# A hand-set order of two engine queues in the middle product of a fused attention and two-MLP kernel: other due times, weight passes queued up to three granules ahead, other sums in the closing chain

## The chip, the cores and the metric

The kernel runs on one core of a Trainium2 chip. Five engines take part, each with a queue that it works through strictly in order: TensorE (PE, matrix products into PSUM), ScalarE (ACT), VectorE (DVE), GpSimd (POOL) and SyncE (SP, which only issues DMAs here). An instruction that waits for a semaphore holds up everything behind it on its engine. The metric is device time in microseconds (us) of one launch; lower is better.

## What is computed

```python
x = attention(q, k, v)                 # 2 x 12 heads, 448 tokens, head size 64, causal, fp32
x = reshape(x)                         # (896 tokens, 768)
y = ((x @ w_a) * (x @ w_b)) @ w_out    # 768 -> 1536 -> 768, the "moe" weights
h = y @ w_in                           # 768 -> 2048, the "moe2" weights
g = h * sigmoid(h)
out = (g @ w_out2).astype(float32)     # 2048 -> 768
```

All is fp32. The kernel keeps that accuracy by splitting each operand into a high and a low part of a narrower type (`fp32r`) and running three matmuls for each product: high x high, high x low, low x high.

## The kernel before

**Stages.** Attention comes first (to about 92 us), then stage 1 (`w_ab`, the two gate products), stage 2 (`w_mid`, the middle product), stage 3 (`w_in`) and stage 4 (`w_out`). A stage is a list of granules; a granule is a pair of 128-column output blocks, named by its first block m, and a plain granule is 72 matmuls long (12 for each of 6 chunks), a fast one 63. A fast granule does the product of a 2x2 block matrix with seven block products instead of eight (Winograd's form): block products 1, 2, 6, 5, 7, 3, 4 in this order, 9 matmuls each, on sums of activations `p1` to `p7` and sums of weights `wa`, `wb`, `wc`, `wd`, each as a high and a low half (`p5h`, `p5l`, `wbh`, `wbl`).

**The middle product** has six granules on PE in this order: plain m=0, plain m=2, fast m=0, plain m=4, fast m=2, fast m=4. Stage 3 follows with fast granules m=0, 2, 4 and on. A plain granule ends with four accumulators (`acc`, one PSUM bank each; there are 8 banks in all). Three of them stay in PSUM until the fast granule of the same m has added its part (`held`), the fourth is copied to SBUF (`o`). In a fast granule of stage 2 (`quad`, lines 897 to 955) block products 1, 6, 7 and 4 pile up in one bank `a`. After 1, after 6 and after 7 ScalarE copies the bank (`s1`, `s2`, `s3`, line 340), and PE may add the next product only when that copy has been made. VectorE adds the other banks to these copies (`plus`, line 921), which sets the banks free. In stage 3, which has no held banks, product 5 is copied as well (`s5`), before product 3 may use its bank.

**Weights.** A granule's weights arrive by two DMAs into three raw buffers `wr`. A raw buffer is loaded again only after VectorE has joined it. Each one passes ScalarE twice (lines 241 and 246) and VectorE once (line 252, `wq`, the join). A fast granule then takes four VectorE sums (lines 300 and 305, `wt`) and four pairs of halves: ScalarE makes the high one (line 274), VectorE the low one (line 278). There is one `wq` and one `wt` buffer, so a join waits for the last reader of the granule before.

**Activations of stage 3.** After fast m=0 and m=2 the sums `p3`, `p5`, `p6`, `p7` are made by `sums_mid` (lines 499 to 549: one sum at line 515, then halves at lines 520 and 521). After fast m=4, the last one, the last third of all `p` is made by `closing` (lines 345 to 395): sums at line 363, high halves on ScalarE at line 352, low halves on VectorE at line 355. Stage 3 m=0 needs it chunk by chunk as the third chunk of each block product.

**What sets the order.** Nothing is scheduled by a compiler here. The program is recorded once, and `Timeline` merges two things onto the ScalarE and VectorE queues: tasks that a product has put there with a delay counted in matmuls (`line.after`), and the weight steps of coming granules, each with a due time in matmuls from a table (`CONV_F`, and the hand-set `MID_2`, `MID_4`, `IN_0`, `IN_2`, `IN_4`). `line.convert` puts the weight steps of granule at+2 on this list when granule `at` begins. A time in the tables is in matmuls relative to the granule's own start (`at_mm`).

## Time and profile before

| what | value |
|---|---|
| median of 3 runs | 550.06 us (549.98 to 550.39) |
| the profiled execution | 550.08 us |
| its span, first to last instruction | 548.3 us |
| mean granted TensorE clock | 0.999 |
| PE busy | 538.6 us, 98% of the span |
| VectorE busy | 427.4 us, 78% |
| ScalarE busy | 388.2 us, 71% |
| middle product on PE (plain m=0 to the start of stage 3) | ends at 328.0 us |

The profile gives for each engine its busy time, the instructions in order of time with the idle time before each and what ended it, and who waited for whom. Matmul ends are modelled, so the idle time shown before a matmul is shorter than what PE lost there. The distance between the starts of neighbouring matmuls is the better measure: where nothing is late, one starts 0.20 us after the other.

### The profile page before, as it was taken

What the parts mean: (1) busy time and instruction counts of PE and PEld (TensorE: products, weight loads), DVE (VectorE), ACT (ScalarE), POOL (GpSimd) and SP (SyncE); (2) the same over time, 40 slices, a digit from 0 to 9 for tenths busy, and PEclk for the clock granted to TensorE, in tenths of its full rate; (3) what the DMA queues carried; (4) which work ended last, traced back from release to release, by engine and by line L of the source; (5) the groups of instructions that cost most, each with busy time, mean ns of one, the idle gap of its engine ahead of it and who ended that gap; (6) DMA issues with size and microseconds to landing.
All of it is one profiled execution on the core that took longest, in us unless ns stands there. A gap on an engine that the chain in (4) does not pass through costs nothing.

```text
span 548.3 us, 8421 instructions
## 1 busy us (share of the span) xinstructions
PE 538.6 (98%) x3016; PEld 469.8 (86%) x3016; DVE 427.4 (78%) x858; ACT 388.2 (71%) x727; POOL 47.8 (9%) x101
## 2 busy tenths in 40 slices
PE   9999999999999999999989998999999999999997
PEld 6566667999999999999978987999999999999996
DVE  5798897987877878999878799877765696475773
ACT  6999986766666666887675657987776897375631
POOL 4565570000000000000000000000000000000000
PEclk9999999999999999999999999999999999999999
DMA  7574340333333334426343303334433233622022
GB/s 224 167 273 120 134 154 3 108 123 115 117 115 116 115 126 139 144 62 205 91 157 116 116 1 109 121 122 137 144 93 139 68 124 104 222 84 91 18 100 86
DMA packets 17226, 65.82 MB, mean 120 GB/s; under 512 B 3616, under 2 KB 5152, under 8 KB 17184
## 3 DMA queue, kind: packets, MB, share of 16 engines
q1 hardware_dynamic: 17184, 65.28, 36.0%
q8 instruction: 24, 0.39, 0.3%
q14 instruction: 18, 0.15, 0.1%
HBM read 62.52 MB, written 2.75 MB: 119 GB/s over the span
## 4 chain that ended last, share of the span: by engine, by line
PE 90%; DVE 5%; ACT 2%; DMA 1%; issue 1%; SPq 0%; ACTq 0%
PE acc L317 77%; PE xo L781 4%; PE pt L770 4%; PE sc L696 3%; PE sc L707 2%; DMA v<-v 1%; DVE s L921 1%; PE wp L799 1%; DVE wq L252 0%; SPq L672 0%; DVE wt L300 0%; DVE S L515 0%; ACT wr L246 0%; ACT wr L241 0%; DVE wal L278 0%
## 5 line engine op out<-in xcount | busy, mean ns | idle before, releaser
L340 ACT COPY s<-acc 128x448 f32<-128x448 f32 x93 | 49.5, 533 | 81.7 <-PE acc L317 81.1
L252 DVE SCALAR_TENSOR_TENSOR wq<-wr 128x768 uint32<-128x768 uint32 (+1 forms) x70 | 65.2, 933 | 20.8 <-ACT wr L246 20.8
L246 ACT ACTIVATE wr<-wr,wbias 128x768 uint32<-128x768 uint32 (+1 forms) x70 | 68.3, 975 | 0.0
L241 ACT ACTIVATE wr<-wr 128x768 f32<-128x768 f32 (+1 forms) x70 | 62.6, 894 | 0.0
L727 ACT ACTIVATE p<-sm,nmax 128x256 f32<-128x256 f32 (+3 forms) x84 | 43.9, 528 | 7.8 <-DVE nmax L722 6.7
L739 POOL TENSOR_SCALAR p<-p,rcp 128x256 f32<-128x256 f32 (+3 forms) x84 | 45.1, 555 | 33.8 <-DVE rcp L736 23.5
L722 DVE CUSTOM_DVE_ANT_0 sm<-sc,mask 128x256 f32<-128x256 f32 (+3 forms) x84 | 30.5, 416 | 7.6 <-PE sc L696 4.5
L913 DVE TENSOR_TENSOR s<-acc,s 128x448 f32<-128x448 f32 x42 | 26.0, 620 | 9.3 <-PE acc L317 9.3
L278 DVE TENSOR_TENSOR wbl<-wt,wbh 128x768 fp32r<-128x768 f32 x24 | 23.0, 957 | 12.0 <-ACT wbh L274 12.0
L278 DVE TENSOR_TENSOR wcl<-wt,wch 128x768 fp32r<-128x768 f32 x24 | 23.0, 956 | 11.5 <-ACT wch L274 11.4
L317 PE MATMUL acc<-th,wgbh 128*128 128x448 f32 x96 | 27.6, 366 | 1.0 <-DVE s L921 1.0
L317 PE MATMUL acc<-th,wgah 128*128 128x448 f32 x96 | 27.6, 367 | 0.8 <-DVE s L921 0.8
L317 PE MATMUL acc<-p6h,wch 128*128 128x448 f32 x72 | 26.5, 367 | 1.4 <-ACT s L340 1.4
L317 PE MATMUL acc<-tl,wgbh 128*128 128x448 f32 x96 | 27.4, 366 | 0.0
L317 PE MATMUL acc<-th,wgal 128*128 128x448 f32 x96 | 27.4, 366 | 0.0
L317 PE MATMUL acc<-tl,wgah 128*128 128x448 f32 x96 | 27.3, 366 | 0.0
L317 PE MATMUL acc<-th,wgbl 128*128 128x448 f32 x96 | 27.3, 366 | 0.0
L305 DVE TENSOR_TENSOR wt<-wq,wt 128x384 f32<-128x384 f32 x48 | 26.6, 555 | 0.8
L770 PEld LDWEIGHTS pt<-ident,p 128*128 128x128 f32 x192 | 20.5, 141 | 7.6 <-POOL p L739 6.0
L770 PE MATMUL pt<-ident,p 128*128 128x128 f32 x192 | 26.7, 280 | 0.3 <-POOL p L739 0.3
L317 PE MATMUL acc<-p3h,wdh 128*128 128x448 f32 x72 | 26.3, 366 | 0.5 <-ACT s L340 0.5
L317 PE MATMUL acc<-p7h,wbh 128*128 128x448 f32 x72 | 26.4, 367 | 0.1
(205 smaller groups left out, 1532.9 us busy)
## 6 DMA issues: line engine op xcount, KB each, us to landing
wr<-w_ab SPq DMA_DIRECT2D x24, 768.0 KB, 4.6
wr<-w_in SPq DMA_DIRECT2D x16, 768.0 KB, 4.5
wr<-w_mid SPq DMA_DIRECT2D x12, 768.0 KB, 4.4
wr<-w_out SPq DMA_DIRECT2D x12, 768.0 KB, 4.8
qk<-qk SPq DMA_DIRECT2D x12, 448.0 KB, 5.0
v<-v SPq DMA_DIRECT2D x12, 256.0 KB, 4.3
wr<-w_out SPq DMA_DIRECT2D x6, 512.0 KB, 4.4
out<-o SPq DMA_DIRECT2D x12, 224.0 KB, 1.9
```

What stands on the lines that cost most here:

```text
L241: nc.scalar.activation(out=w, in_=w, func=AF.Prelu, scale=2.0 ** -112, alpha=-(2.0 ** 32))
L246: nc.scalar.activation(out=word(i, 0), in_=word(i, 0), func=AF.Relu, bias=wbias, scale=2.0 ** -29)
L252: nc.vector.scalar_tensor_tensor(out=xi(i), in0=word(i, 1), scalar=3, in1=word(i, 0), op0=ALU.logical_shift_left, op1=ALU.bitwise_or)
L278: nc.vector.tensor_tensor(out=view[1], in0=src(), in1=view[0].bitcast(F32), op=ALU.subtract)
L305: nc.vector.tensor_tensor(out=sums(1, k), in0=tile(1 - k, 1), in1=sums(k, 0), op=ALU.subtract)
L317: nc.tensor.matmul(out=acc[:, 0:S], lhsT=w, rhs=a, start=first, stop=last, skip_group_check=True)
L340: nc.scalar.copy(out=t, in_=acc[:, 0:S])
L722: nc.vector.tensor_tensor_reduce(out=sm[:, o:o + m.shape[-1]], in0=sc, in1=m, op0=ALU.add, op1=ALU.min, scale=-(D ** -0.5), scalar=nmax, a ...
L727: nc.scalar.activation(out=p_sb[u % 2][j][:, 0:K], in_=sm[:, 0:K], func=AF.Exp, bias=t["nmax"][:, c:c + 1], scale=-1.0, accum_out=t["sums" ...
L739: nc.gpsimd.tensor_scalar(out=pj, in0=pj, scalar1=t["rcp"][:, COL[j]:COL[j] + 1], scalar2=1.0, op0=ALU.mult, op1=ALU.mult,)
L770: nc.tensor.transpose(out=out_, in_=p, identity=ident)
L913: nc.vector.tensor_tensor(out=t, in0=bank[:, 0:S], in1=other, op=ALU.add)
```

## The change

Three parts, all in how the two queues are filled; no arithmetic instruction is added or removed except that one sum of the closing chain goes another way, with the same count of instructions on every engine.

1. The due times of five weight tables are other ones, and plain m=4 of stage 2 gets a table of its own (`MID_P`).
2. The weight steps of stage 3 m=0 and m=2 are queued up to three granules ahead (`ahead`) instead of two.
3. `sums_mid` makes the sums in another order (S1, S2, S3, S4), and the halves with them. In `closing` three sums stood between the last copy and S2's first half (held part to s3, s3 minus s1, held part off s1); now the held part is taken off s1 as soon as s1 is there, s3 minus s1 follows alone, and the held part goes to s3 at the end.

```diff
-MID_2 = at_mm(72, exp=(-52, -34), low=(-48, -30), join=(-24, -20), t13=-16, t24=-12,
-              wa=(-14, -8), wd=(-10, -5), wc=(-6, 0), wb=(2, 6))
+MID_P = at_mm(63, exp=(-20, -12), low=(-15, -8), join=(-7, -2), ghi=(0, 4), glo=(5, 9))
+MID_2 = at_mm(72, exp=(-50, -42), low=(-46, -34), join=(-40, -29), t13=-24, t24=-16,
+              wa=(-13, -4), wd=(-9, 4), wc=(1, 10), wb=(5, 14))
...
             if (i, j) == (0, 0):
+
+                def part_of():
+                    op(t, t, h[3], ALU.subtract)
                 line.after(3, partial(halves_of, t, 1))
+                line.after(8, part_of)
             elif (i, j) == (0, 1):
-                halves_of(t, 2, 2)
+                f["rest2"] = halves_of(t, 2, None)
             elif (i, j) == (1, 1):
-                halves_of(t, 4)
-
-                def ahead():
-                    a11, part = f[0, 0], h[3]
-                    op(t, part, t, ALU.add)
-                    f["S2"] = A.new(F32, "S")
-                    op(f["S2"], t, a11, ALU.subtract)
-                    op(a11, a11, part, ALU.subtract)
-                    A.free(part)
-                line.after(6, ahead)
+                f["S2"] = A.new(F32, "S")
+                op(f["S2"], t, f[0, 0], ALU.subtract)
+                f["rest"] = halves_of(t, 4, None)
             else:
                 op(s2, src, s2, ALU.add)
                 r6 = halves_of(s2, 6, None)
+                f["rest2"]()
+                r6()
+                op(s3, s3, src, ALU.subtract)
+                f["rest"]()
+                op(s1, s1, h[3], ALU.add)
+                A.free(h[3])
                 op(s1, src, s1, ALU.add)
-                op(s3, s3, src, ALU.subtract)
                 banks.free(t)
-                r6()
                 op(s4, s4, s2, ALU.subtract)
...
+        if g["stage"] == 2 and not g["fast"] and g["m"] == NP - 2:
+            g["due"] = MID_P
+        if g["stage"] == 3 and g["m"] < 4:
+            g["ahead"] = True
...
-            if at + 2 < len(granules):
-                line.convert(granules[at + 2], used - LEAD, granules[at + 1]["length"])
+            ends = used
+            for n in (2, 3):
+                if at + n < len(granules):
+                    if "queued" not in granules[at + n] and (n == 2 or granules[at + n].get("ahead")):
+                        granules[at + n]["queued"] = True
+                        line.convert(granules[at + n], ends - LEAD, granules[at + n - 1]["length"])
+                    ends += granules[at + n - 1]["length"]
```

**Place 1.** VectorE in fast m=0, where its sums set the four banks free that plain m=4 begins with (`s1`, `s2`, `s3` lines: the copies that take the banks in; `wq`, `wt`: weights of fast m=2). Before:

```order
L252 SCALAR_TENSOR_TENSOR wq_3316<-wr_3102 128x768
L252 SCALAR_TENSOR_TENSOR wq_3316<-wr_3222 128x768
L921 TENSOR_TENSOR s2_3294<-acc_3277,s2_3294 128x448
L300 TENSOR_TENSOR wt_3335<-wq_3316 128x3x128 x2
L305 TENSOR_TENSOR wt_3335<-wq_3316,wt_3335 128x3x128 x2
L921 TENSOR_TENSOR s3_3330<-acc_3277,s3_3330 128x448
L921 TENSOR_TENSOR s3_3330<-acc_2973,s3_3330 128x448
L278 TENSOR_TENSOR wal_3342<-wq_3316,wah_3341 128x768
L278 TENSOR_TENSOR wdl_3352<-wq_3316,wdh_3351 128x384
L921 TENSOR_TENSOR s2_3294<-acc_2972,s2_3294 128x448
```

The same stretch in the changed kernel:

```order
L253 SCALAR_TENSOR_TENSOR wq_3293<-wr_3102 128x768
L927 TENSOR_TENSOR s1_3272<-acc_2970,s1_3272 128x448
L253 SCALAR_TENSOR_TENSOR wq_3293<-wr_3213 128x768
L1017 TENSOR_TENSOR p1l_3311<-s1_3272,p1h_3310 128x448
L301 TENSOR_TENSOR wt_3323<-wq_3293 128x3x128 x2
L927 TENSOR_TENSOR s2_3301<-acc_3285,s2_3301 128x448
L306 TENSOR_TENSOR wt_3323<-wq_3293,wt_3323 128x3x128 x2
L927 TENSOR_TENSOR s3_3333<-acc_3285,s3_3333 128x448
L927 TENSOR_TENSOR s3_3333<-acc_2973,s3_3333 128x448
L279 TENSOR_TENSOR wal_3344<-wq_3293,wah_3343 128x768
L927 TENSOR_TENSOR s2_3301<-acc_2972,s2_3301 128x448
```

The two joins stand earlier, one of them ahead of the first sum, and the last bank's sum now comes ahead of `wdl`.

**Place 2.** ScalarE from fast m=4 to stage 3 m=0 (`s1_3640`, `s2_3683`, `s3_3719`: copies that PE waits for in fast m=4; `s1_3773` the first one of stage 3; `p..h` high halves for stage 3). Before:

```order
L520 CAST p5h_3653<-S_3648 128x448
L274 CAST wbh_3666<-wt_3581 128x768
L520 CAST p7h_3674<-S_3660 128x448
L340 COPY s2_3683<-acc_3625 128x448
L352 CAST p1h_3689<-s1_3640 128x448
L520 CAST p6h_3695<-S_3680 128x448
L520 CAST p3h_3711<-S_3702 128x448
L340 COPY s3_3719<-acc_3625 128x448
L352 CAST p4h_3732<-s3_3719 128x448
L352 CAST p2h_3739<-s2_3683 128x448
L352 CAST p6h_3755<-S_3748 128x448
L340 COPY s1_3773<-acc_3762 128x448
```

The same stretch in the changed kernel:

```order
L522 CAST p6h_3679<-S_3653 128x448
L341 COPY s2_3683<-acc_3625 128x448
L353 CAST p1h_3690<-s1_3640 128x448
L522 CAST p7h_3702<-S_3669 128x448
L522 CAST p3h_3712<-S_3688 128x448
L341 COPY s3_3720<-acc_3625 128x448
L242 ACTIVATE wr_3433<-wr_3433 128x768
L247 ACTIVATE wr_3433<-wr_3433,wbias_58 128x768
L353 CAST p4h_3737<-s3_3720 128x448
L353 CAST p2h_3744<-s2_3683 128x448
L353 CAST p6h_3754<-S_3735 128x448
L341 COPY s1_3775<-acc_3764 128x448
```

`p6h` has moved ahead of the copy s2 and `p7h` behind it, and a weight pass stands between s3 and the closing halves.

**Place 3.** VectorE in the closing chain, up to the high half `p6h`'s sum (`S_...`) and on. Before:

```order
L355 TENSOR_TENSOR p4l_3733<-s3_3719,p4h_3732 128x448
L355 TENSOR_TENSOR p2l_3740<-s2_3683,p2h_3739 128x448
L363 TENSOR_TENSOR s3_3719<-o_3520,s3_3719 128x448
L363 TENSOR_TENSOR S_3748<-s3_3719,s1_3640 128x448
L363 TENSOR_TENSOR s1_3640<-s1_3640,o_3520 128x448
L363 TENSOR_TENSOR S_3748<-acc_3625,S_3748 128x448
L363 TENSOR_TENSOR s3_3719<-acc_3625,s3_3719 128x448
L363 TENSOR_TENSOR s1_3640<-s1_3640,acc_3625 128x448
L355 TENSOR_TENSOR p6l_3756<-S_3748,p6h_3755 128x448
L363 TENSOR_TENSOR s2_3683<-s2_3683,S_3748 128x448
L355 TENSOR_TENSOR p5l_3779<-s3_3719,p5h_3778 128x448
```

The same stretch in the changed kernel:

```order
L364 TENSOR_TENSOR S_3735<-s3_3720,s1_3640 128x448
L927 TENSOR_TENSOR s2_3683<-acc_3371,s2_3683 128x448
L364 TENSOR_TENSOR S_3735<-acc_3625,S_3735 128x448
L356 TENSOR_TENSOR p2l_3745<-s2_3683,p2h_3744 128x448
L356 TENSOR_TENSOR p6l_3755<-S_3735,p6h_3754 128x448
L364 TENSOR_TENSOR s1_3640<-s1_3640,acc_3625 128x448
L356 TENSOR_TENSOR p4l_3738<-s3_3720,p4h_3737 128x448
L364 TENSOR_TENSOR s3_3720<-s3_3720,o_3524 128x448
L364 TENSOR_TENSOR s3_3720<-acc_3625,s3_3720 128x448
L364 TENSOR_TENSOR s2_3683<-s2_3683,S_3735 128x448
L356 TENSOR_TENSOR p5l_3783<-s3_3720,p5h_3782 128x448
```

The two sums that `p6h` rests on (`S`) stood behind `p4l`, `p2l` and the held part's sum (`o_3520`); now they stand ahead of these, with one sum that frees a bank (`s2`) between them.

## Rows read from the trace of the kernel before

**Rows 1.** The page: busy us (share of span) of the engines.

```profile
PE 538.6 (98%) x3016; PEld 469.8 (86%) x3016; DVE 427.4 (78%) x858; ACT 388.2 (71%) x727; POOL 47.8 (9%) x101
```

**Rows 2.** Waits of PE: line waited for, us in total, times, longest.

```profile
PE acc L317 <- ACT s L340: 2.1, 3, 1.4
PE acc L317 <- DVE s L921: 1.9, 2, 1.0
```

**Rows 3.** Stretches: start:end, us, busy us (x instructions) by engine, PE clock, DMA.

```profile
271.74:343.46 71.72, 67.66 (x326) 60.49 (x325) 59.21 (x97) 44.36 (x71) 0.00 (x0) 1.00 0.29 100
```

**Rows 4.** Timeline of PE: start us, us, instruction; around the six late matmuls.

```profile
284.51 0.37 PE L317 MATMUL acc<-th,wgah 128*128 128x448 f32 x1
...
286.00 0.56 PE L317 MATMUL acc<-tl,wgah 128*128 128x448 f32 x2
...
286.81 0.36 PE L317 MATMUL acc<-th,wgbh 128*128 128x448 f32 x1
...
288.52 0.57 PE L317 MATMUL acc<-tl,wgbh 128*128 128x448 f32 x2
...
321.49 0.37 PE L317 MATMUL acc<-p5h,wbl 128*128 128x448 f32 x1
...
322.24 0.37 PE L317 MATMUL acc<-p7l,wbh 128*128 128x448 f32 x1
...
325.48 0.36 PE L317 MATMUL acc<-p3h,wdl 128*128 128x448 f32 x1
...
326.38 0.36 PE L317 MATMUL acc<-p4l,wch 128*128 128x448 f32 x1
...
331.45 0.37 PE L317 MATMUL acc<-p2h,wal 128*128 128x448 f32 x1
...
333.55 0.36 PE L317 MATMUL acc<-p6l,wch 128*128 128x448 f32 x1
...
338.65 0.37 PE L317 MATMUL acc<-p7h,wbl 128*128 128x448 f32 x1
...
339.81 0.36 PE L317 MATMUL acc<-p3l,wdh 128*128 128x448 f32 x1
```

**Rows 5.** Timeline of VectorE (DVE): weight sums, two chained sums, unchained work.

```profile
283.02 1.02 DVE L300 TENSOR_TENSOR wt<-wq 128x384 f32<-128x384 f32 x2
...
285.02 1.28 DVE L921 TENSOR_TENSOR s<-acc,s 128x448 f32<-128x448 f32 x2
...
320.63 0.62 DVE L521 TENSOR_TENSOR p5l<-S,p5h 128x448 fp32r<-128x448 f32 x1
321.17 0.95 DVE L278 TENSOR_TENSOR wbl<-wt,wbh 128x768 fp32r<-128x768 f32 x1
322.04 0.62 DVE L515 TENSOR_TENSOR S<-S,s 128x448 f32<-128x448 f32 x1
```

**Rows 6.** Timeline of ScalarE (ACT): copies (L340) and what stands around them.

```profile
277.40 0.54 ACT L340 COPY s<-acc 128x448 f32<-128x448 f32 x1
...
279.09 1.00 ACT L246 ACTIVATE wr<-wr,wbias 128x768 uint32<-128x768 uint32 x1
...
319.68 0.57 ACT L520 CAST p5h<-S 128x448 fp32r<-128x448 f32 x1 [1.32 <-DVE S L515]
...
332.19 0.56 ACT L352 CAST p6h<-S 128x448 fp32r<-128x448 f32 x1 [3.08 <-DVE S L363]
...
338.44 0.58 ACT L1025 ACTIVATE s<-s 128x448 f32<-128x448 f32 x1
338.93 0.95 ACT L340 COPY s<-acc 128x448 f32<-128x448 f32 x2
...
346.08 0.51 ACT L340 COPY s<-acc 128x448 f32<-128x448 f32 x1
```

**Rows 7.** DMA issue near 281.8, then one at 295.0 us: median us to landing.

```profile
wr<-w_mid SPq DMA_DIRECT2D x1, 768.0 KB, 4.6
...
wr<-w_in SPq DMA_DIRECT2D x1, 768.0 KB, 6.1
```

More of the change, by code (lines that the diff above doesn't have):

```diff
@@ L67, in at_mm @@
             else (due[name] + LEAD) / length for name in due}
-MID_2 = at_mm(72, exp=(-52, -34), low=(-48, -30), join=(-24, -20), t13=-16, t24=-12,
-              wa=(-14, -8), wd=(-10, -5), wc=(-6, 0), wb=(2, 6))
-MID_4 = at_mm(63, exp=(-62, -54), low=(-58, -50), join=(-44, -40), t13=-36, t24=-32,
+MID_P = at_mm(63, exp=(-20, -12), low=(-15, -8), join=(-7, -2), ghi=(0, 4), glo=(5, 9))
+MID_2 = at_mm(72, exp=(-50, -42), low=(-46, -34), join=(-40, -29), t13=-24, t24=-16,
+              wa=(-13, -4), wd=(-9, 4), wc=(1, 10), wb=(5, 14))
+MID_4 = at_mm(63, exp=(-68, -58), low=(-64, -52), join=(-52, -46), t13=-42, t24=-38,
               wa=(0, 4), wc=(2, 8), wd=(5, 11), wb=(19, 23))
-IN_0 = at_mm(63, exp=(-53, -35), low=(-49, -31), join=(-44, -26), t13=-22, t24=-18,
-             wa=(-16, -12), wd=(-3, 0), wc=(1, 4), wb=(19, 22))
-IN_2 = at_mm(63, exp=(10, 28), low=(14, 32), join=(18, 36), t13=40, t24=44,
+IN_0 = at_mm(63, exp=(-94, -84), low=(-90, -80), join=(-50, -46), t13=-38, t24=-33,
+             wa=(-16, -12), wd=(-13, -8), wc=(1, 4), wb=(19, 22))
+IN_2 = at_mm(63, exp=(-17, 10), low=(-16, 11), join=(28, 34), t13=40, t24=44,
              wa=(46, 50), wd=(48, 54), wc=(54, 60), wb=(60, 66))
-IN_4 = at_mm(63, exp=(-7, 10), low=(-3, 14), join=(2, 18), t13=28, t24=33,
+IN_4 = at_mm(63, exp=(-14, 10), low=(-13, 14), join=(2, 18), t13=28, t24=33,
              wa=(30, 38), wd=(34, 44), wc=(42, 50), wb=(48, 56))
@@ L386, in put @@
                 r6 = halves_of(s2, 6, None)
+                f["rest2"]()
[4 more added lines that the diff above has]
+                A.free(h[3])
                 op(s1, src, s1, ALU.add)
-                op(s3, s3, src, ALU.subtract)
                 banks.free(t)
-                r6()
                 op(s4, s4, s2, ALU.subtract)
                 A.free(s2)
-                line.after(10, partial(halves_of, s1, 5, 3, True))
+                line.after(12, partial(halves_of, s1, 5, 3, True))
                 line.after(14, partial(halves_of, s3, 7, 4, True))
@@ L524, in sums_mid @@
         s1 = add(a21, a22, ALU.add)
+        yield 1
+        s2 = add(s1, a11, ALU.subtract)
         yield 2
-        rest = halves_of(s1, 5)
+        r5 = halves_of(s1, 5)
         yield 1
@@ L530, in sums_mid @@
         yield 0
-        rest()
+        r5()
         yield 2
-        rest = halves_of(s3, 7)
-        yield 1
-        s2 = add(s1, a11, ALU.subtract)
-        yield 0
-        rest()
-        A.free(s3)
-        yield 2
-        rest = halves_of(s2, 6)
+        r6 = halves_of(s2, 6)
         yield 1
@@ L543, in sums_mid @@
         yield 0
-        rest()
+        r6()
+        A.free(s1, s2, a11, a12, a22)
         yield 2
-        rest = halves_of(s4, 3)
+        r7 = halves_of(s3, 7)
         yield 0
-        rest()
-        A.free(s1, s2, s4, a11, a12, a22)
+        r7()
+        yield 2
+        r3 = halves_of(s4, 3)
+        yield 0
+        r3()
+        A.free(s3, s4)
     class Sums:
```

## The prediction, made before the changed kernel was run

> **What bounds the kernel now.** The page comes first: PE is busy for 98% of the span and no other engine for more than 78% [rows 1]. So the kernel is as long as PE's own work plus what PE loses while it waits, and the list of PE's waits shows who makes it lose: the copies on ScalarE, 2.1 us in three waits, and the bank sums on VectorE, 1.9 us in two [rows 2]. All of these lie between 271.74 us (start of fast m=0) and 343.46 us (second matmul of stage 3 m=2), where PE's clock is granted in full, 2.4 GHz, VectorE is busy for 59.2 of 71.7 us and ScalarE for 44.4 [rows 3].
>
> The idle times are too short for what was lost, since matmul ends are modelled, so I measure from start to start. Undisturbed, fast m=0 puts 63 matmuls into 284.51 - 271.74 = 12.77 us, 0.203 us each [rows 3, 4]. At a late matmul the stretch from the one ahead to the one behind it holds two such steps, 0.41 us. The six stretches [rows 4]: 286.00 - 284.51 = 1.49, loss 1.08; 288.52 - 286.81 = 1.71, loss 1.30 (plain m=4 begins, two banks not yet free); 322.24 - 321.49 = 0.75, loss 0.34 (fast m=4, product 7 waits for the copy s2); 326.38 - 325.48 = 0.90, loss 0.49 (product 4, copy s3); 333.55 - 331.45 = 2.10, loss 1.69 (stage 3 m=0, product 6, copy s1); 339.81 - 338.65 = 1.16, loss 0.75 (product 3, copy s5). Together 5.65 us. That is all that a new order of the two queues can give back; it removes no work from PE.
>
> **A price that the rows deny.** After a late matmul the granted clock stays at 1.00 [rows 3], and the second and third matmul after it are back at the old distance (two in 0.56 us at 286.00, where one takes 0.36 [rows 4]), so a wait costs its length and about 0.1 us of restart, both in the 5.65. By the Trainium skill (Perfetto Trace Analysis, "Matmul Optimizations") TensorE scales its power with its use, so that matmuls should run back to back. By that each wait would cost clock as well and the gain would be above 5.65; the trace does not agree here.
>
> **The change, part by part.** I lay the changed order out on the two queues, on the clock of before, with PE undisturbed: plain m=4 from 284.5, fast m=2 from 284.51 + 72 x 0.203 = 299.1, fast m=4 from 311.9, stage 3 m=0 from 324.7, m=2 from 337.5. From start to start a VectorE sum or low half of 448 columns takes 321.17 - 320.63 = 0.54, one of 768 columns 322.04 - 321.17 = 0.87 (a join too), a sum that needs the one right ahead of it about 0.65, since two such take 1.28 with the last end [rows 5].
>
> *Place 1, plain m=4's banks.* The last input from ScalarE is the second pass of the second raw buffer; it follows the copy s2 (277.40) and ends 0.43 + 1.00 later, 278.83 [rows 6]. Then VectorE does: join 0.87, p1l 0.54, four weight sums 285.02 - 283.02 = 2.00 [rows 5] with the sum s2 among them 0.54, s3 plus b 0.65 (end 283.5; PE needs the bank at 284.7), s3 plus d 0.54 (end 284.1; needed at 285.7), `wal` 0.87, s2 plus e (end 278.87 + 0.87 + 0.54 + 2.00 + 0.54 + 0.65 + 0.54 + 0.87 + 0.62 = 285.5; needed at 284.51 + 7 x 0.203 = 285.9). Before, both joins and `wgbl` stood behind p1l and `wdl` ahead of the last sum. Gain 1.08 + 1.30; the least margin is 0.4 us.
>
> *Place 2, copies s2 and s3 of fast m=4.* The copy s2 was late because `p5h` waited 1.32 us for a sum on VectorE [rows 6] with `wbh` and `p7h` behind it. Now weights of stage 3 m=0 are joined during fast m=2, and `p6h`, whose sum is made second, is what stands before the copy. Anchored at the copy s3 of fast m=2 (PE's product 7 ends near 308.5, copy to 309.1, `wah` to 309.9, its 0.8 estimated from the 0.87 of a low half of that size), VectorE has, up to `p6h`'s sum: `wal` 0.87, s3 twice 0.65 + 0.54, `wdl` with half the columns 0.47, s2 0.54, p4l 0.54, `wcl` 0.97 with a short wait, the held sum, S1's and S2's three chained ones 3 x 0.65: end 316.4. `wbh` and `p6h` take 1.2 more, 317.5, and PE releases the copy at 317.6: it is made at once, and PE needs it at 319.2. The copy s3 follows `p3h` in the same way. Gain 0.34 + 0.49, margin over 0.8 us.
>
> *Place 3, the closing chain and copy s1.* `p6h` waited 3.08 us for its sum and the copy s1 stood behind it [rows 6]. Now one chained sum stands ahead of that sum's last step instead of three, and it ends 17 VectorE operations after 316.2: one of 0.87, three chained 1.95, 12 others 6.48, the last 0.62, together 9.9, at 326.1; `p6h` to 326.7; the copy, released by PE at 326.8, ends near 327.4, needed at 324.71 + 18 x 0.203 = 328.4. Gain 1.69, margin 1 us.
>
> *Copy s5.* It stands behind a Silu that needs stage 3's first sum. From 316.2, right behind that sum of place 2, VectorE has 28 operations up to that sum without a hole: one of 768 columns 0.87, five chained 3.25, 21 others 11.34, the last 0.62, together 16.1, end 332.3; with two short waits for ScalarE up to 332.6. Silu 0.49 (338.93 - 338.44), copy 0.54 [rows 6]: 333.3 to 333.7, needed at 324.71 + 45 x 0.203 = 333.8. Gain 0.75, margin only 0.1 to 0.5 us.
>
> *What is late next.* The first copy of m=2. In m=0's last third ScalarE now has passes ahead of `wch`, and VectorE's `wcl` and the sum s2 behind that one: the same eleven ScalarE instructions, from the copy s3 to the end of this one, took 7.2 us before (second copy of the pair at 338.93, from 339.34, to 346.08 + 0.51), 0.5 of it a wait [rows 6]. From 334.1, where PE releases the copy s3, that is 340.8 to 341.3; it is needed at 337.5 + 18 x 0.203 = 341.2. I take 0.1 us of loss; bounds 0 and 0.5 (the copy's whole length).
>
> *Edits at no cost.* Queuing three granules ahead, `MID_P` and the new `sums_mid` move only work that the two engines hold between PE's marks above; the cover is ScalarE's slack, 66.1 - 44.4 = 22 us once the 5.65 are gone from the 71.7, and VectorE's, 66.1 - 59.2 = 7 us [rows 3]. If VectorE's cover is gone, the last two margins go first. From stage 3 m=2 on both orders are the same.
>
> **Sum.** 550.08 (profiled execution, 0.02 from the median 550.06) - 5.65 + 0.1 = 544.5 us.
>
> **Rivals.**
>
> *A, the thin margins fail.* VectorE has no hole from about 310 to 337 us, and copy s5 and m=2's first copy have 0 to 0.5 us. If the 28 operations run 3 to 10% longer or two more chained waits appear, s5 is late by 0.3 to 1.5 us and m=2's copy by as much again, and the last bank of place 1 may add 0.5: 0.6 to 3 us of the gain is lost, 545.1 to 547.5. For it: several releases that I take from ScalarE are within 0.1 us of their need. Against it: a late PE gives the slack back at once. By the Trainium skill (VectorE: DVE Perf Modes, "The DRAIN you can't avoid") a VectorE operation waits for the pipe to empty anyway, and a chain with semaphores takes as long as one without; then the five chained sums of the 28 would cost 0.54 each, s5 would be 0.5 us earlier and A less likely. The rows do not agree: 0.65 against 0.54 [rows 5], so I keep A's chance.
>
> *B, it ends slower.* A pass of one raw buffer of stage 3 m=0 stands on ScalarE ahead of `p7h`, and its load can be issued only when VectorE has joined an earlier buffer, near 291.2 us. ScalarE is there at 292.6 and waits with all of fast m=2's copies behind it. A load lands after 4.6 us, the second of a close pair after 6.1 [rows 7]: 295.8 to 297.3. The first copy behind it is needed at 302.8, and some 5.5 us of ScalarE work stand between (two passes, five high halves and two copies, the last included), so PE loses nothing up to about 297.3 and from then on one us for each us. It ends slower than before only if it loses 5.65 + 1.1 us, that is if the load takes 13 us or more: 551.2 to 553. No row shows that.
>
> *C, it does not do what it says.* Each wait is only handed on: PE runs into the next late copy as soon as it is not held by the one before, since VectorE's 59 us of work per 66 us of PE [rows 3] would already be the limit. Then 548.5 to 551.2. Against it: 7 us of hole are left, 10%, and the places above fit.
>
> **How the numbers follow.** Forecast 0.62 (543.9 to 545.1), A 0.24 (545.1 to 547.5), C 0.07, B 0.07. 0.2% of 550 is 1.1 us, about what a measurement of this kernel can tell from no change. Faster by more than that: the forecast, A and the lower part of C (0.02), 0.88. Within: the rest of C, 0.05. Slower: B, 0.07. The range holds the forecast and most of A: 543.9 to 546.8.
>
> **What would show it.** Right: in the changed trace PE has no wait of over 0.2 us between fast m=0 and stage 3 m=2, and 324 matmuls (fast m=0 to the end of m=0 of stage 3) take about 66 us instead of 71.5; ScalarE idles some 3 us near 293 us for a load and PE does not notice. Wrong: a late product 3 or 6 at stage 3's start (A), a copy s1 late in fast m=2 (B), or PE's waits as many as before in other places (C). The tail from stage 3 m=2 on must be as long as before; if it is not, I have missed something outside of the middle product.

## The result, and the profile after

The changed kernel takes 544.97 us (median of 4 runs, 544.94 to 545.18) where the kernel before takes 550.02 (4 runs, 549.53 to 550.39): a ratio of 0.991, 95% interval 0.989 to 0.993. The forecast was 544.5, its range 543.9 to 546.8. The profiled execution took 544.95 us with a span of 543.2; its page gives, as busy us (share of span) and chain of waits by engine:

```profile
PE 537.2 (99%) x3016; PEld 470.1 (87%) x3016; DVE 427.1 (79%) x858; ACT 388.6 (72%) x727; POOL 47.8 (9%) x101
...
PE 97%; DMA 1%; SPq 0%; DVE 0%; issue 0%
```

VectorE and ScalarE are as busy as in [rows 1]; only the time in which PE waited is gone. The list of PE's waits in the changed kernel (line waited for, us in total, times, longest) has no row with `acc` left, where [rows 2] had five waits:

```profile
PE wp L805 <- DVE wz L802: 1.1, 1, 1.1
PE xo L787 <- DMA v<-v: 0.9, 1, 0.9
PE pt L776 <- POOL p L745: 0.3, 1, 0.3
```

What the change touches lies between the first matmul of fast m=0 and the first of stage 3 m=4, 387 matmuls. The windows of that stretch (start:end, us, then busy us of each engine, clock, DMA), first before and then after:

```profile
271.74:356.09 84.35, 80.29 (x389) 72.13 (x387) 69.88 (x112) 56.01 (x89) 0.00 (x0) 1.00 0.31 103
```

```profile
271.94:350.72 78.78, 78.78 (x388) 72.58 (x387) 69.42 (x112) 55.70 (x89) 0.00 (x0) 1.00 0.30 105
```

84.35 - 78.78 = 5.57 us; the prediction's sum for this stretch was 5.65 - 0.1 = 5.55. PE is now busy from the first to the last of it. The next 378 matmuls, the last steady quads of stage 3, hold the same instructions in both kernels and yet take longer, again before and then after:

```profile
356.09:432.81 76.72, 76.72 (x380) 70.98 (x378) 51.66 (x78) 58.82 (x99) 0.00 (x0) 1.00 0.34 114
```

```profile
350.72:427.65 76.93, 76.93 (x380) 70.99 (x378) 51.82 (x78) 58.93 (x99) 0.00 (x0) 1.00 0.34 113
```

That is 0.21 us given back, and another 0.20 was lost ahead of it all: fast m=0 begins at 271.94 instead of 271.74, because a load of `v` at the kernel's start landed later (PE's wait for it 0.9 us, 0.7 before). -5.57 + 0.21 + 0.20 = -5.16, and the two profiled executions differ by 544.95 - 550.08 = -5.13; the 0.03 between these lie behind the quads or in rounding.

The start scatters: over all kernels run here fast m=0 begins anywhere from 270.72 to 272.83 us, in the same instructions, so that medians of four runs differ by some tenths without a reason in the change. The changed kernel and e6 and e14 below show it: their spans between the same matmuls agree to 0.03 us, their medians are 544.97, 544.63 and 544.64. The experiments are therefore read by two spans that no start reaches: the **middle** (the 387 matmuls above) and the **quads** (the 378). A wait is given as the step from one matmul's start to the next, less the 0.204 us of an undisturbed step; the matmul behind the wait then takes 0.1 us longer, once.

### The profile page after: what moved, and what is told of

The parts are those of the page before. It is cut to its first block, busy times and chain, and to the rows that moved or that the text cites. A ratio compares the mean times of both kernels' runs of the same rounds, so it can differ in the third digit from the quotient of the medians.

```text
span 543.2 us, 8418 instructions
## 1 busy us (share of the span) xinstructions
PE 537.2 (99%) x3016; PEld 470.1 (87%) x3016; DVE 427.1 (79%) x858; ACT 388.6 (72%) x727; POOL 47.8 (9%) x101
## 4 chain that ended last, share of the span: by engine, by line
PE 97%; DMA 1%; SPq 0%; DVE 0%; issue 0%
PE acc L318 84%; PE xo L787 4%; PE pt L776 4%; PE sc L702 3%; PE sc L713 2%; DMA v<-v 1%; PE wp L805 1%; SPq L678 0%; DVE o L1045 0%; SPq L675 0%; DVE wz L802 0%
## 5 line engine op out<-in xcount | busy, mean ns | idle before, releaser
L318 PE MATMUL acc<-p5l,wbh 128*128 128x448 f32 x72 | 26.4, 366 | 0.0
L318 PE MATMUL acc<-p7h,wbl 128*128 128x448 f32 x72 | 26.3, 366 | 0.0
```

What stands on the lines that cost most here:

```text
L318: nc.tensor.matmul(out=acc[:, 0:S], lhsT=w, rhs=a, start=first, stop=last, skip_group_check=True)
```

## The experiments

All of them, in us. The two spans are each from one profiled execution:

| kernel | median | ratio to before, 95% | middle | quads |
|---|---|---|---|---|
| before | 550.02 | | 84.35 | 76.72 |
| after | 544.97 | 0.989 to 0.993 | 78.78 | 76.93 |
| e1, old `MID_2` | 546.13 | 0.990 to 0.994 | 80.17 | 76.96 |
| e2, old `sums_mid` | 544.62 | 0.987 to 0.992 | 78.94 | 76.72 |
| e3, old closing chain | 545.53 | 0.989 to 0.993 | 79.41 | 76.96 |
| e10, old `sums_mid` and closing chain | 544.93 | 0.989 to 0.993 | 79.65 | 76.72 |
| e11, old `IN_0` | 546.62 | 0.992 to 0.996 | 80.42 | 76.93 |
| e4, before with the new closing chain | 550.64 | 0.999 to 1.002 | 86.08 | 76.72 |
| e7, ScalarE later in fast m=4 | 548.38 | 0.996 to 0.998 | 82.94 | 76.96 |
| e7b, ScalarE later behind the load | 545.90 | 0.991 to 0.995 | 80.24 | 76.96 |
| e8, VectorE later in stage 3 m=0 | 545.96 | 0.990 to 0.995 | 80.03 | 76.96 |
| e6, no third granule ahead | 544.63 | 0.989 to 0.992 | 78.79 | 76.96 |
| e14, other buffers, same order | 544.64 | 0.988 to 0.992 | 78.79 | 76.96 |
| e13, old `sums_mid`, `v` loaded first | 543.89 | 0.987 to 0.990 | 78.91 | 76.72 |

### e1: the old order of the weights of fast m=2

```
-MID_2 = at_mm(72, exp=(-50, -42), low=(-46, -34), join=(-40, -29), t13=-24, t24=-16,
-              wa=(-13, -4), wd=(-9, 4), wc=(1, 10), wb=(5, 14))
+MID_2 = at_mm(72, exp=(-52, -34), low=(-48, -30), join=(-24, -20), t13=-16, t24=-12,
+              wa=(-14, -8), wd=(-10, -5), wc=(-6, 0), wb=(2, 6))
```

> The changed kernel with the old due times of fast m=2 (MID_2) alone. Theory (place 1: the two joins of fast m=2 have to stand ahead of the bank sums in VectorE's queue): with both joins behind p1l and wdl ahead of the last bank's sum, the sum s3 plus b still ends at its need, but s2 plus e ends near 287.4 where plain m=4 needs it at 286.15, so one bank wait of 1.2 to 1.4 us comes back and nothing else: 546.2 to 546.5 us. Rival (the banks came late because of the weights of plain m=4, wgal and wgbl, which another table moved): no wait comes back, 545.0 us. Rival (the table is the whole of place 1): both waits come back, 2.4 us, 547.4 us.

Measured: the middle 1.39 us longer. The timeline of PE (start us, us, instruction, idle time before it and what ended it) shows one bank wait back, at plain m=4:

```profile
286.65 0.36 PE L318 MATMUL acc<-th,wgbh 128*128 128x448 f32 x1
288.05 0.47 PE L318 MATMUL acc<-th,wgbh 128*128 128x448 f32 x1 [1.04 <-DVE s L927]
```

The step is 1.40, the loss 1.20 and 0.1 of restart. This is the second bank of [rows 4] (286.81 to 288.52). The first bank only just misses its matmul: it costs a restart of 0.09 and no wait, which is the rest of the 1.39.

### e2 and e10: the old order of the plain sums, and of both chains

e2 has `sums_mid` of the kernel before, e10 its closing chain as well. The core of e2's diff, in `sums_mid`:

```
-        yield 1
-        s2 = add(s1, a11, ALU.subtract)
         yield 2
-        r5 = halves_of(s1, 5)
+        rest = halves_of(s1, 5)
...
-        r6 = halves_of(s2, 6)
+        rest = halves_of(s3, 7)
+        yield 1
+        s2 = add(s1, a11, ALU.subtract)
...
```

> The changed kernel with the old order of sums in sums_mid alone. What the prediction said of place 2 (p6h, made second, is what now stands before the copy s2, so the new order frees the copies s2 and s3): the two waits of fast m=4 come back, 0.34 + 0.49 = 0.83 us, 545.8 us. Rival (the earlier joins of stage 3 m=0 free VectorE, and the order of the sums has no part in it): laid out again, p7h is ready near 317.6 and p3h near 322.3, both before PE needs the copies behind them; only the closing chain starts 0.15 us later, 0 to 0.2 us, 545.0 to 545.2 us.

> The changed kernel with the order of sums_mid and of the closing chain as they were before; the four tables, the early weights of stage 3 and the three granules ahead stay. Theory 1 (the tables and the early joins free VectorE in fast m=4 and give nearly all): the two waits that the old closing chain alone brought back return, 0.59 at product 6 of stage 3 m=0 and 0.16 at the first copy of m=2, and nothing else; 0.5 to 0.8 us above the changed kernel, 545.4 to 545.9. Theory 2 (either of the two orders covers for the other, so that each looks free when it alone is undone): the waits of fast m=4 and the long one of copy s1 come back, 0.34 + 0.49 + 1.69 = 2.5 us, 547.5 and more.

Measured: e2 loses nothing in fast m=4; only the copy at m=2 is 0.1 us later (the middle is 0.16 longer), and the quads are 0.21 shorter, so that e2 ends where the changed kernel does. e10 loses 0.87 in the middle, 0.85 of it in one wait of copy s1 and its restart (328.12 to 329.07) and the rest at m=2, and gets the 0.21 back. Neither order covers for the other: what [rows 4] lost in fast m=4 does not return with both undone. The tables and the early weights give 5.57 - 0.87 = 4.70 us of the 5.57 by themselves (the early queuing has no part in it, see e6).

### e3 and e4: the closing chain, undone alone and put in alone

e3 is the changed kernel with the old chain; e4 is the kernel before with the new one, the same lines the other way round:

```
-                f["S2"] = A.new(F32, "S")
-                op(f["S2"], t, f[0, 0], ALU.subtract)
-                f["rest"] = halves_of(t, 4, None)
+                halves_of(t, 4)
+
+                def ahead():
+                    a11, part = f[0, 0], h[3]
+                    op(t, part, t, ALU.add)
+                    f["S2"] = A.new(F32, "S")
+                    op(f["S2"], t, a11, ALU.subtract)
+                    op(a11, a11, part, ALU.subtract)
+                    A.free(part)
+                line.after(6, ahead)
...
```

> The changed kernel with the old closing chain alone. The prediction (place 3: the chain two sums shorter is what frees the copy s1 of stage 3 m=0) in its plain reading: product 6 of stage 3 m=0 waits 1.7 us again, 546.7 us. Rival (the chain's start moved as well, since VectorE has less in front of it): the old chain ends near 327.9, p6h at 328.5, the copy s1 at 328.9 where PE needs it at 328.65: a wait of 0.3 to 0.5 us there and perhaps 0.1 to 0.3 at the first copy of m=2, 545.4 to 545.8 us.

> The kernel before with the new closing chain alone. If the chain's length is the cause of the wait for the copy s1 (1.69 us), it goes and the two bank waits (2.4 us) and the two of fast m=4 (0.8 us) stay; the copy s5 is then needed 1.69 us earlier and its wait of 0.75 us grows, by up to 0.7. So 548.3 to 549.0 us. Rival (the queues in front of the chain are the cause): p6h stays late, 549.5 to 550.0 us.

Measured for e3: the middle 0.63 longer. PE waits once for the copy s1 of stage 3 m=0:

```profile
329.35 0.37 PE L318 MATMUL acc<-p2h,wal 128*128 128x448 f32 x1
330.04 0.47 PE L318 MATMUL acc<-p6h,wch 128*128 128x448 f32 x1 [0.32 <-ACT s L341]
```

a loss of 0.49 and 0.1, not the 1.69 of the kernel before. For e4 the middle is 1.73 us longer than before, although its wait for copy s1 is gone. Its timeline of PE around plain m=4, and the windows that follow:

```profile
283.50 0.37 PE L317 MATMUL acc<-th,wgah 128*128 128x448 f32 x1
284.68 0.47 PE L317 MATMUL acc<-th,wgah 128*128 128x448 f32 x1 [0.81 <-DVE s L922]
...
285.80 0.36 PE L317 MATMUL acc<-th,wgbh 128*128 128x448 f32 x1
287.20 0.60 PE L317 MATMUL acc<-th,wgbh 128*128 128x448 f32 x1 [1.04 <-DVE s L922]
```

```profile
287.10:290.70 3.60, 3.50 (x10) 3.11 (x11) 3.56 (x7) 3.16 (x5) 0.00 (x0) 0.54 0.00 0
290.70:297.00 6.30, 6.30 (x33) 5.83 (x32) 6.23 (x11) 2.35 (x4) 0.00 (x0) 0.99 0.52 155
```

The two bank waits are those of the kernel before, but behind the second the granted clock is 0.54, the 1.2 GHz level: 10 matmuls where 3.6 us hold 18 at full clock. Plain m=4 takes 1.54 us longer than before by it. Without that the middle would be 0.19 longer than before: the copy s3 of fast m=4 is later than it was (a step of 1.24 us at product 4, before 0.59), the second copy of stage 3 m=0 is late at product 7, where nothing was (1.18), and the copy s5 at product 3 a little more (1.02, before 0.85). So in the old order each wait is only handed on, as rival C had it. Neither reading of the expectation had that: both put e4 at 550.0 us or below, the median is 550.64. The fallen clock is not the rule in e4: its profiled execution is one of two in ten runs with a mean granted clock of 0.997, the other eight are at 0.999 or 1.0.

### e11: the old order of the weights of stage 3 m=0

```
-IN_0 = at_mm(63, exp=(-94, -84), low=(-90, -80), join=(-50, -46), t13=-38, t24=-33,
-             wa=(-16, -12), wd=(-13, -8), wc=(1, 4), wb=(19, 22))
+IN_0 = at_mm(63, exp=(-53, -35), low=(-49, -31), join=(-44, -26), t13=-22, t24=-18,
+             wa=(-16, -12), wd=(-3, 0), wc=(1, 4), wb=(19, 22))
```

> The changed kernel with the old table of stage 3 m=0 alone (its weights joined during fast m=4 as before, and the load wait on ScalarE gone). Theory 1 (the joins taken out of fast m=4 are what frees VectorE there): two joins and one low half of 0.87 with ScalarE's passes stand among the sums again, the waits at products 7 and 4 of fast m=4 and at product 6 of stage 3 m=0 come back at least in part, 1.0 to 2.5 us above the changed kernel, 546.0 to 547.5. Theory 2 (this table has no part, the shorter chain and the earlier weights of fast m=4 are enough): within 0.3 us, 544.7 to 545.3.

Measured: the middle 1.64 us longer. Its timeline of PE in fast m=4 and in stage 3 m=0:

```profile
319.15 0.37 PE L318 MATMUL acc<-p5h,wbl 128*128 128x448 f32 x1
319.58 0.47 PE L318 MATMUL acc<-p7h,wbh 128*128 128x448 f32 x1
...
332.15 0.44 PE L318 MATMUL acc<-p5h,wbh 128*128 128x448 f32 x1
332.77 0.47 PE L318 MATMUL acc<-p5l,wbh 128*128 128x448 f32 x1 [0.18 <-DVE p5l L356]
```

Product 7 of fast m=4 loses 0.23 + 0.11 = 0.34, just what [rows 4] lost there. Most of the rest is lost a granule later in stage 3 m=0: 0.22 at product 2 and 0.52 at product 5, both on low halves from VectorE, and 0.29 at product 7, on ScalarE's second copy, which ends at 333.42 behind casts that waited for VectorE. No wait comes back at the copies s3 and s1 ([rows 4], products 4 and 6). The expectation put the joins into fast m=4. They stand in fast m=2 (which begins at 299.25 here), as in the kernel before, but later than in the changed kernel; the timeline of VectorE in e11:

```profile
303.50 0.96 DVE L253 SCALAR_TENSOR_TENSOR wq<-wr 128x768 uint32<-128x768 uint32 x1 [1.98 <-ACT wr L247]
...
307.63 0.96 DVE L253 SCALAR_TENSOR_TENSOR wq<-wr 128x768 uint32<-128x768 uint32 x1 [0.28 <-ACT wr L247]
```

The low halves of these weights follow 1.3 to 2.6 us later than in the changed kernel, three of them in fast m=4, ahead of the closing chain.

### e7 and e7b: ScalarE made later, to measure how much is covered

In both the cast `p7h` is repeated behind itself; e7 does it seven times for `c == 1`, e7b five times for `c == 0`:

```
         r7 = halves_of(s3, 7)
+        if c == 1:
+            for _ in range(7):
+                nc.scalar.copy(out=ACTS[3][7][c][0], in_=s3)
```

> The changed kernel with the cast p7h of the last plain sums made seven times more on ScalarE (the same values again), right behind the pass that waits for the load: 7 x 0.46 = 3.2 us that end where a load would end that lands 3.2 us later, at 299.1 instead of 295.9. By rival B's arithmetic the cover is 1.1 to 1.6 us (copy s1 of fast m=2 ends at 301.94 after 0.38 of idle time and is needed near 303.1) and from there on every us counts: 1.6 to 2.1 us above the changed kernel, 546.6 to 547.1, all of it at fast m=2's first copies. If ScalarE's slack takes it up (22 us of it between fast m=0 and stage 3 m=2), 0 to 0.3 us: 545.0 to 545.3.

> The changed kernel with the cast p7h that stands behind the load wait on ScalarE (298.25 us there) made five times more, the same values again. Such repeats stood 0.60 us apart in the run before this one, so ScalarE is 3.0 us later, as by a load that lands 3.0 us later. Rival B's mechanism: in the changed kernel copy s1 of fast m=2 follows 0.38 us of idle time and ends at 301.94, and PE needs it 18 matmuls after 299.39, at 303.06; so 0.38 + 1.1 = 1.5 us are covered and the rest, 1.5 us with 0.1 of restart, is lost at product 6 of fast m=2: 546.3 to 546.7 us, more only if the clock falls behind the wait, as it did behind a wait of 2.5 us. The other view, that ScalarE's slack of some 22 us takes it up: within 0.2 us, 544.8 to 545.2.

e7's casts did not stand where its expectation put them: `c == 1` is the pair of fast m=4. So e7 measures the margin of place 2. The timelines of ScalarE and then of PE there:

```profile
319.78 4.15 ACT L547 CAST p7h<-S 128x448 fp32r<-128x448 f32 x7
...
324.30 0.53 ACT L341 COPY s<-acc 128x448 f32<-128x448 f32 x1
```

```profile
322.20 0.37 PE L318 MATMUL acc<-p3h,wdl 128*128 128x448 f32 x1
324.88 0.47 PE L318 MATMUL acc<-p4h,wch 128*128 128x448 f32 x1 [2.31 <-ACT s L341]
```

From the start of fast m=4 (311.41 here, 312.17 in the changed kernel) the copy s3 is at 12.89 us instead of 9.36, 3.53 later; PE loses 2.68 - 0.20 = 2.48. The margin was 1.05 us. And here too the clock falls behind the wait in the profiled execution (five of the ten runs of e7 have a mean granted clock of 0.997), 12 matmuls in 3.4 us:

```profile
325.30:328.70 3.40, 3.40 (x12) 2.98 (x11) 3.23 (x7) 2.37 (x4) 0.00 (x0) 0.53 0.02 5
328.70:335.00 6.30, 6.30 (x32) 5.84 (x31) 5.96 (x12) 4.71 (x8) 0.00 (x0) 0.98 0.00 0
```

which, with the restart, makes up the rest of the 4.16 us by which the middle is longer.

e7b's casts stand behind the load, with the copies of fast m=2 behind them. Timelines of ScalarE and PE:

```profile
297.12 2.96 ACT L547 CAST p7h<-S 128x448 fp32r<-128x448 f32 x5
...
302.76 0.53 ACT L341 COPY s<-acc 128x448 f32<-128x448 f32 x1
```

```profile
301.79 0.36 PE L318 MATMUL acc<-p2h,wal 128*128 128x448 f32 x1
303.35 0.47 PE L318 MATMUL acc<-p6h,wch 128*128 128x448 f32 x1 [1.20 <-ACT s L341]
```

Counted from the start of fast m=2, ScalarE's copy `o` ahead of them is 2.88 us later than in the changed kernel; of these PE loses 1.36 and 0.1 of restart; the middle is 1.46 longer, near the 1.6 expected, and the clock stays. So 2.88 - 1.36, some 1.5 us, were covered, as worked out ahead from the idle time and the copy's need. That one us costs one from there on is laid out from the queue's order; one length of delay cannot show it.

### e8: VectorE made later in stage 3 m=0

```
                 f["rest2"]()
+                for _ in range(2):
+                    f["rest2"]()
                 r6()
```

> The changed kernel with the low half p2l of stage 3 m=0 made two times more on VectorE (the same values again), behind the closing chain's sum for p6h: 2 x 0.54 = 1.08 us in front of stage 3's first sum, on which the Silu ahead of the copy s5 waits. If VectorE's queue is the bound there (its margin for the copy s5 is 0 to 0.1 us, and no hole follows), the loss is 0.95 to 1.2 us, 545.9 to 546.2, at product 3 of stage 3 m=0, and the first copy of m=2 is handed on no further loss, since PE gives it the same time. If the margin is what rival A's sum counted as a hole (the idle time of VectorE further back), nothing: 544.9 to 545.2.

Measured: the middle 1.25 longer. The repeats took 0.66 each, 1.32 in all, since each writes what the one before it wrote. Almost all of it reaches PE, but not at product 3 as the expectation had it: the timeline of PE shows the low half of product 5 late, then product 7. With the restarts that is 0.54 and 0.30; 0.17 went at product 2 ahead of them, 0.09 at product 3 and 0.16 at the first copy of m=2 behind them.

```profile
332.42 0.44 PE L318 MATMUL acc<-p5h,wbh 128*128 128x448 f32 x1
333.05 0.47 PE L318 MATMUL acc<-p5l,wbh 128*128 128x448 f32 x1 [0.19 <-DVE p5l L356]
333.36 0.36 PE L318 MATMUL acc<-p5h,wbl 128*128 128x448 f32 x1
333.75 0.47 PE L318 MATMUL acc<-p7h,wbh 128*128 128x448 f32 x1
```

Product 7 waits for ScalarE: its second copy of the granule ends at 333.17 + 0.53 = 333.70, behind three casts, the first of which waited for a sum on VectorE. The timeline of ScalarE:

```profile
331.77 0.57 ACT L353 CAST p5h<-s 128x448 fp32r<-128x448 f32 x1 [1.96 <-DVE s L364]
...
333.17 0.53 ACT L341 COPY s<-acc 128x448 f32<-128x448 f32 x1
```

### e6, e14, e13: the third granule, the buffers, and the best version

e6 takes out the two lines that set `g["ahead"]`. e14 moves where `sums_mid` gives its buffers back, and changes no instruction and no order:

```
-        A.free(s1, s2, a11, a12, a22)
...
-        A.free(s3, s4)
+        A.free(s2, s1, s3, s4, a11, a12, a22)
```

e13 is e2 with the first load of `v` moved:

```
             load_qk(2)
+            load_v(0)
...
-                if i == 0 and 0 < u <= NU:
+                if i == 0 and 1 < u <= NU:
```

> The changed kernel without the third granule ahead: the passes of stage 3's first weights are queued one granule later, and the cast p7h no longer stands behind the load. Theory (both orders hide this work): no wait of PE changes, within 0.15 us of the changed kernel, 544.8 to 545.2. Rival (the early passes are what frees ScalarE in fast m=4): the copies s2 and s3 of fast m=4 are late again, 0.3 to 0.9 us, 545.3 to 545.9.

> The changed kernel with the buffers of sums_mid given back at its end instead of halfway. No instruction and no order on any engine changes; only half of stage 3's products lie in other buffers of SBUF. Theory 1 (the pace of the steady quads of stage 3 hangs on which buffers the operands lie in): the 378 matmuls of the last steady quads, 76.93 us in the changed kernel and 76.72 with the old order of sums_mid, take another time, 76.6 to 77.1, and not 76.93 within 0.02. Theory 2 (it hangs on the order of the instructions): 76.93 +- 0.02. The whole time either way 544.7 to 545.3.

> The changed kernel with two edits: the old order of sums_mid, and the first load of v issued ahead of the two big weight loads of the start. Old sums_mid: the 378 matmuls of the last steady quads of stage 3 take 76.7 us in every run that has it and 76.9 in every run that has the new one, 0.2 us in all of stage 3. v first: its landing held PE for 0.7 to 1.6 us and was the start's scatter of 2 us; issued at 6 us instead of 10 it should land near 11 to 13, and the wait goes. Theory: 0.2 + 0.7 to 0.9 us below the changed kernel, 543.9 to 544.1, with less scatter, and the fastest of all. Rival: the weight loads land later by as much as v takes, and the first weights hold stage 1 instead: 0.2 us below the changed kernel or as long, 544.6 to 545.0.

e6: the middle 78.79, no change. Without the third granule ScalarE's queue has no load wait there, and nothing is worse for it.

e14: the quads take 76.96, within 0.03 of the changed kernel's. That is outside of the 0.02 which its expectation allowed, but e1, e3, e6, e7, e7b and e8 show the same 76.96; it is no sign of the buffers. The six granules of the quads explain both figures: each takes 12.79 us with the old order of `sums_mid` and 12.83 with the new one, the 0.04 in its first 21 matmuls, and in the changed kernel and e11 the first of the six still takes 12.79. That half of the products lie elsewhere in e14 is read from the code; the traces hold no addresses.

e13: 543.89 us, 0.75 below e6 and e14, which ran with it on the same chip; its interval to before, 0.987 to 0.990, overlaps with theirs. The wait for `v` is gone from its list of PE's waits, and its quads are 76.72. But that wait is absent from the traces of seven other runs too (e2, e4, e6, e7, e7b, e10, e14), in which `v` was not moved, so one trace does not show that the edit took it away. Its profiled execution is its longest, 544.98, with a fast m=0 that begins at 272.07: against the kernel before, 1.14 us come at the first score products, before `v` is read, and e6, whose start is untouched, shows 0.57 there. That part of the start's scatter was not followed up. e13 is the lowest median of all kernels run, by less than the intervals can settle.

## Why the prediction was right, point by point

*The sum.* 5.55 us were forecast between fast m=0 and stage 3 m=4, 5.57 came, and the 324 matmuls that were to take about 66 us took 65.86. The 0.42 us by which the profiled 544.95 lies above the sum before rounding (544.53) are the start (0.20), which varies, and the quads (0.21), of which the prediction said that both orders are the same from stage 3 m=2 on. From m=4 on the order is the same on PE, ScalarE and VectorE, the time is not: by the prediction's own last sign it missed something outside of the middle product, and what it is stays open. The rival A, whose band begins at 545.1, is not what cost it. The sum needs only that all six waits go. It does not depend on what takes them away, and at places 2 and 3 that was in part something else than the prediction said; there the number is better than its reasons.

*Place 1.* The last bank sum ends in the changed kernel at 285.06 + 0.62 = 285.68, on a clock 0.2 later than that of before, where 285.5 was laid out; its room is the 0.4 us that the prediction gave it (needed at 286.15). The timeline of VectorE has it, and two sums of the later places:

```profile
285.06 0.62 DVE L927 TENSOR_TENSOR s<-acc,s 128x448 f32<-128x448 f32 x1
...
325.60 0.61 DVE L364 TENSOR_TENSOR S<-acc,S 128x448 f32<-128x448 f32 x1
...
332.11 0.62 DVE L919 TENSOR_TENSOR s<-acc,s 128x448 f32<-128x448 f32 x1
```

e1 confirms the place for the second bank.

*Place 2: the gain came, its reason falls.* The step that failed is "`p6h`, whose sum is made second, is what stands before the copy". With the old order of the sums (e2) both copies are on time as well. What the runs put in its place is near the other half of that paragraph, "now weights of stage 3 m=0 are joined during fast m=2", but not as it stands. The times in a table count from the start of the granule ahead (`line.convert` adds them to `used`, the start of granule `at` + 1, for granule `at` + 2), and not from the granule's own start, as the section on the kernel before has it. So those of `IN_0` count from fast m=4, and the joins stood in fast m=2 already. The timeline of VectorE before, where fast m=2 begins at 301.56, and then in the changed kernel, where it begins at 299.39:

```profile
305.82 0.96 DVE L252 SCALAR_TENSOR_TENSOR wq<-wr 128x768 uint32<-128x768 uint32 x1 [1.95 <-ACT wr L246]
...
309.98 0.96 DVE L252 SCALAR_TENSOR_TENSOR wq<-wr 128x768 uint32<-128x768 uint32 x1 [0.28 <-ACT wr L246]
```

```profile
301.88 1.83 DVE L253 SCALAR_TENSOR_TENSOR wq<-wr 128x768 uint32<-128x768 uint32 x2
```

So the second join comes 8.42 us behind the start of fast m=2 before, and 3.4 in the changed kernel, and the weights' low halves in fast m=4 follow sooner. Undone (e11), product 7's 0.34 us return. What keeps copy s3 on time was not found: neither e11 nor e10 brings its 0.49 back, and `MID_4` alone was not undone. The margin, "over 0.8 us", is 1.05 (e7).

*Place 3: the same, in part.* The closing sum was laid out to end at 326.1 and ends at 326.21, the copy s1 is on time. (The layout of place 3 and of copy s5 starts from 316.2, where the one of place 2 ends at 316.4; the sum of S2 that it means ends at 316.43.) But of the 1.69 us only 0.6 hang on the shorter chain (e3), or 0.85 on it and the order of the sums together (e10): the rest was gone with the due times alone. Which table took it away is not shown; e11 brings no wait at the copy s1 back. The chain alone (e4) does free the copy s1, as the prediction had it, and the time is lost again at the other copies.

*Copy s5 and the copy behind it.* The timeline of ScalarE in the changed kernel: copy s1, the Silu, copy s5, and the first copy of m=2:

```profile
327.03 0.53 ACT L341 COPY s<-acc 128x448 f32<-128x448 f32 x1 [0.21 <-PE acc L318]
...
332.76 0.58 ACT L1031 ACTIVATE s<-s 128x448 f32<-128x448 f32 x1 [0.93 <-DVE s L919]
333.25 0.52 ACT L341 COPY s<-acc 128x448 f32<-128x448 f32 x1
...
340.91 0.53 ACT L341 COPY s<-acc 128x448 f32<-128x448 f32 x1
```

Copy s5 ends at 333.77 (333.3 to 333.7 laid out). The copy of m=2 ends at 341.44 (340.8 to 341.3 laid out) and costs 0.1 us, as taken; the timeline of PE shows the matmul that just misses it:

```profile
341.25 0.37 PE L318 MATMUL acc<-p2h,wal 128*128 128x448 f32 x1
341.48 0.47 PE L318 MATMUL acc<-p6h,wch 128*128 128x448 f32 x1
341.79 0.36 PE L318 MATMUL acc<-p6l,wch 128*128 128x448 f32 x1
```

Copy s5 has the least room ahead of it, as the prediction said: it ends 0.36 us before the matmul that needs it (334.13), and a matmul that waits starts 0.05 behind its copy, which leaves 0.31, inside the 0.1 to 0.5 laid out. What the prediction and the expectation of e8 left out is that a late VectorE meets PE before that. Worked out in the same way, the low half of product 5 (ends at 331.13, needed at 331.91) has some 0.7 us of room and the second copy (331.84, 332.31) some 0.4; whatever PE loses there (e8, e11) it no longer loses at s5.

*Rival B* was laid out rightly and did not decide. ScalarE waits 3.09 us for the load, and the copies of fast m=2 are made in time:

```profile
291.92 1.00 ACT L247 ACTIVATE wr<-wr,wbias 128x768 uint32<-128x768 uint32 x1
296.02 0.91 ACT L242 ACTIVATE wr<-wr 128x768 f32<-128x768 f32 x1 [3.09 <-DVE S L517]
...
301.41 0.53 ACT L341 COPY s<-acc 128x448 f32<-128x448 f32 x1 [0.38 <-PE acc L318]
```

The row names a VectorE sum as what ended it, but that sum ends only at 296.02, when the pass begins; it is the load, issued at 291.49 and landed 4.4 us later, at 295.91 (4.6 in [rows 7]), and the one issued behind it at 292.32 took 6.6. The DMA rows, us to landing last:

```profile
wr<-w_in SPq DMA_DIRECT2D x1, 768.0 KB, 4.4
```

```profile
wr<-w_in SPq DMA_DIRECT2D x1, 768.0 KB, 6.6
```

PE would lose from a landing at 295.9 + 1.5 = 297.4 on (an estimate from e7b); the prediction said 297.3. *Rival C* holds for the old order (e4), not for the new.

*"A price that the rows deny"* was drawn too widely from one execution. That no wait costs clock is true of the profiled one; the profiled execution of e4, with the same two bank waits at the same place, fell to the 1.2 GHz level behind them. Of the 33 runs of the kernel before that stand beside the experiments, eight have a mean granted clock of 0.997 and took 550.70 to 552.32 us; the other 25, at 0.999 or 1.0, took 549.31 to 550.88. By the Trainium skill (Perfetto Trace Analysis, "Matmul Optimizations") TensorE scales its power with its use. The profiled executions of e4 and e7 agree with that; those of before, e1 and e7b do not show it. So the forecast left out a cost that falls on some runs of the kernel before. Whether the change takes it away is not shown: its four runs are at 1.0, but so are most runs of the kernel before, and one run each of e13 and e14 is at 0.998.

## What to carry to other kernels

Where one engine is the bound and waits many times for queues that are nearly full, lay the new order out operation by operation, with the time at which the bound engine needs each result: the sum came out to 0.02 us, because what each of the six waits cost was measured from start to start, and all six went. Which edit earned it is a different question, and only undoing them one by one tells: here the due times of the weights, not the shorter chain, gave most (4.70 of 5.57 us), and the chain alone nothing, since a full queue hands each wait on. Even that is not the whole: the single parts undone here cost 1.39, 1.64, 0.63, 0.16 and 0.01 us in the middle, 3.83 together, and `MID_P`, `MID_4`, `IN_2` and `IN_4` were not undone by themselves. Before comparing medians of a few tenths, cut the kernel's own scatter out, with a span between two of the same instructions.

## What the runs showed of the hardware

- *The clock after waits.* One wait of 1.2 to 1.4 us (e1, e7b) left the granted clock at full. In the profiled executions of e4 and e7, two of 0.98 and 1.20 us with 1.1 us of matmuls between them (e4), or one of 2.48 (e7), were followed by eight steps of 0.37 us from matmul to matmul instead of 0.20, a granted clock of 0.53 to 0.54, and a loss of some 1.5 us. The two waits of the same size in the profiled execution of before were not, and eight of ten runs of e4 and five of ten of e7 kept a mean granted clock of 0.999 or 1.0.
- *The pace of the same matmuls.* 378 matmuls without a wait took 76.72 us in the five kernels with the old order of `sums_mid` and 76.93 or 76.96 in the nine with the new one, whatever else differed, though that order lies ahead of them and their own order is the same. Giving the buffers back at another place (e14) did not change it. The cause is open.
- *Repeats into one buffer.* A ScalarE cast that writes what the one before it wrote starts 0.60 us after it, where others follow after 0.47; a VectorE low half after 0.66 instead of 0.54.
